# A cap of three on the loads in flight, in a decode kernel of two attention and two feed-forward layers

## The chip, the core and the metric

One core of a Trainium2 chip. The metric is the device time of one execution in microseconds (us). Compared are fast runs with fast runs; a run is called slow when it is more than 1.5% above the fastest of the same kernel. Runs that were made once only are of unknown state, and are used only for differences far above that.

## The reference, cut to what matters

```python
B, Sq, D = 4, 1, 512;  Hq, Hkv, Sk, Dh = 32, 8, 4096, 128;  F = 1792
x = x + A(layernorm(x))   # attention over k_cache, v_cache (B, Hkv, Sk, Dh), bf16
x = x + Bf(layernorm(x))  # (gelu(x @ w_gate) * (x @ w_up)) @ w_down
x = x + A(layernorm(x))   # the same caches and weights again
x = x + Bf(layernorm(x))
```

One token for each of four sequences. Each (sequence, kv head) has 1 MB of K and 1 MB of V, 64 MiB in all. There is little arithmetic on each byte, so the kernel is a stream of loads with matmuls behind it.

## The kernel before

The kernel loads K once per sequence and keeps it, turned (transposed), on the chip for both layers; V is loaded twice. That makes 64 K loads and 128 V loads of 512 KB, and 13.9 MB of weights: 114.6 MB, or 218 times 512 KB. All loads are issued in program order on one queue, that of the sync engine (SP). K and V share one pool of seven buffers, and that pool is all that limits how many K and V loads are in flight (the weights have room of their own).

```python
KV_BUFS = 7
kvin = ctx.enter_context(tc.tile_pool(name="kvin", bufs=KV_BUFS))
dq = nc.sync

def load_kv(cache, b, kvh, t, name):
    tl = kvin.tile([P, CH, Dh], BF16, name=name, tag="kv")        # 128 x 2048 bf16, 512 KB
    src = cache[b, kvh].rearrange("(p c) d -> p c d", p=P)
    dq.dma_start(out=tl[:], in_=src[:, t * CH:(t + 1) * CH])
    return tl
# ... (cut)
v = load_kv(A_v_cache, self.b, kvh, t, "v_t")
for i in range(CH):                                               # 16 matmuls per V load
    c = t * CH + i
    nc.tensor.matmul(o, lhsT=v[:, i, :], rhs=pe[:, s, c, :],
                     start=(c == 0), stop=(c == C - 1))
```

Of the kernel before, what the change touches and what calls it, by code (L numbers as in the profile page):

```python
# [15 lines left out]
P = 128  # L16
# [3 lines left out]
CH = 16  # L20
# [3 lines left out]
NB = 2  # L24
BE = 2 * NB
KV_BUFS = 7


@with_exitstack
def kernel(  # L30
# [14 lines left out]
    B, Sq, D = A_x.shape  # L45
    _, Hkv, Sk, Dh = A_k_cache.shape
    HqDh = A_wq.shape[1]
    Hq = HqDh // Dh
# [9 lines left out]
    HG = GH * rep  # L58
# [6 lines left out]
    ktp = ctx.enter_context(tc.tile_pool(name="ktp", bufs=Hkv))  # L65
    kvin = ctx.enter_context(tc.tile_pool(name="kvin", bufs=KV_BUFS))
    qbp = ctx.enter_context(tc.tile_pool(name="qbp", bufs=2))
# [20 lines left out]
    for a in range(QD):  # L88
        nc.vector.tensor_copy(
            out=sel[:, :, :, a, :],  # L90
            in_=ident_bf[:].rearrange("p (b i e) -> p b e i", b=NB, e=2))
# [4 lines left out]
    wq_sb = wts.tile([P, KD, HqDh], BF16, name="wq_sb")  # L96
    wo_sb = wts.tile([P, Hq, D], BF16, name="wo_sb")
    wg_sb = wts.tile([P, KD, F], BF16, name="wg_sb")
    wu_sb = wts.tile([P, KD, F], BF16, name="wu_sb")
    wd_sb = wts.tile([P, KF, D], BF16, name="wd_sb")  # L100
    wq_dram = A_wq.rearrange("(k p) n -> p k n", p=P)
    wo_dram = A_wo.rearrange("(i p) n -> p i n", p=P)
# [6 lines left out]
    xn_bf = state.tile([P, KD, B], BF16, name="xn_bf")  # L109

    dq = nc.sync


    def load_kv(cache, b, kvh, t, name):
        tl = kvin.tile([P, CH, Dh], BF16, name=name, tag="kv")
        src = cache[b, kvh].rearrange("(p c) d -> p c d", p=P)
        dq.dma_start(out=tl[:], in_=src[:, t * CH:(t + 1) * CH])
        return tl


# [118 lines left out]
    class Turner:  # L239
# [3 lines left out]
        def step(self):  # L243
            kvh, t = divmod(self.n, NT)
            self.n += 1
            if t == 0:
                self.kt = ktp.tile([P, G8, NB, QD, QS], FP32, name="kt", tag="kt")
                KT[kvh] = self.kt
            gt = CH // QD
            kn = load_kv(A_k_cache, self.b, kvh, t, "k_t")  # L250
            kf = kn.rearrange("p c d -> p (c d)").bitcast(FP32).rearrange(
                "p (c b i) -> p c b i", b=NB, i=QS)
            for bb in range(NB):
                nc.vector.transpose(  # L254
                    out=self.kt[:, t * gt:(t + 1) * gt, bb].rearrange("p g c j -> p g (c j)"),
                    in_=kf[:, :, bb])
# [54 lines left out]
    class Values:  # L311
# [3 lines left out]
        def step(self, count=1):  # L315
            for _ in range(count):
                if self.n == Hkv * NT:
                    return
                kvh, t = divmod(self.n, NT)
                self.n += 1  # L320
                s = kvh % GH
                if self.whole:
                    if kvh == 0 and t == 0:
                        self.ot = ps_acc.tile([P, Hkv, rep], FP32, name="ot2", tag="acc")
                    o = self.ot[:, kvh]
                else:
                    if s == 0 and t == 0:
                        self.ot = ps_ot.tile([P, GH, rep], FP32, name="ot", tag="ot")
                    o = self.ot[:, s]
                pe = self.prob[kvh // GH]  # L330
                v = load_kv(A_v_cache, self.b, kvh, t, "v_t")
                for i in range(CH):
# [3 lines that stand above are left out]
# [5 lines left out]

    def rest_weights(i):
        if i == 0:
            dq.dma_start(out=wq_sb[:, :, HG * Dh:2 * HG * Dh], in_=wq_dram[:, :, HG * Dh:2 * HG * Dh])
        elif i == 1:
            dq.dma_start(out=wq_sb[:, :, 2 * HG * Dh:], in_=wq_dram[:, :, 2 * HG * Dh:])
        elif i == 2:
            dq.dma_start(out=wo_sb[:, :Hq // 2], in_=wo_dram[:, :Hq // 2])
        elif i == 3:
            dq.dma_start(out=wo_sb[:, Hq // 2:], in_=wo_dram[:, Hq // 2:])  # L350
            dq.dma_start(out=wg_sb[:], in_=B_w_gate.rearrange("(k p) n -> p k n", p=P))
        elif i == 4:
            dq.dma_start(out=wu_sb[:], in_=B_w_up.rearrange("(k p) n -> p k n", p=P))
            dq.dma_start(out=wd_sb[:], in_=B_w_down.rearrange("(k p) n -> p k n", p=P))


    def attend(b2, qb2, b1, qb1, rstd1):
# [13 lines left out]
        for g in range(NG + 1):  # L371
# [14 lines left out]
            if b1 == 0:  # L386
                rest_weights(g)
                if more:
                    q_norm(q_proj(0, B, g * HG, HG), q1_bf[:, g * HG:(g + 1) * HG], rstd1, HG, B)
# [60 lines left out]


    x_bf = kvin.tile([P, D], BF16, name="x_bf", tag="kv")
    dq.dma_start(out=x_bf[:B, :], in_=A_x.flatten_outer_dims())
    hq0 = HG * Dh
    dq.dma_start(out=wq_sb[:, :, :hq0], in_=wq_dram[:, :, :hq0])

    xT_ps = ps_misc.tile([P, KD, B], BF16, name="xT_ps", tag="misc")
    for k in range(KD):
# [98 lines left out]
```

## Time and profile before

| | before |
|---|---|
| time, median of 3 runs (lowest to highest) | 367.79 us (366.8 to 371.84) |
| the profiled run, slow | 375.1 us, span 373.3 us |
| bytes read | 114.56 MB, 307 GB/s over the span |
| idle TensorE time before value matmuls that waited for V | 60.1 us |
| idle TensorE time called "issue" | 43.4 us |

The page of the kernel before follows. In its lines PE is TensorE, DVE is VectorE, ACT is ScalarE, POOL is GpSimd and SPq is the queue of SP; L334 is line 334 of the kernel. The trace holds 3210 landing marks, 16 for each of the 200 loads of K, V and weights; a load is counted as landed at its last mark. The parts of the page are: the busy share of the 16 DMA engines in 40 slices and the rate of each slice; the DMA queues with packets, MB and their share of the engines' time; the chain of waits by engine and by line; groups of instructions (count, busy us, mean ns, then the engine's idle time before them and what ended it); and the loads with KB and the median us from issue to landing.

```profile
span 373.3 us, 14915 instructions
...
DMA  7999999995078799999879899998888799984730
GB/s 237 421 417 383 416 375 417 395 407 228 11 253 302 234 376 363 382 313 359 288 244 386 347 329 377 358 341 275 271 332 308 265 382 413 345 311 147 248 119 2
...
q1 hardware_dynamic: 36240, 114.58, 83.7%
q8 instruction: 53, 0.87, 0.9%
...
PE 38%; DMA 29%; issue 16%; DVE 15%; POOL 1%; ACT 1%; SPq 0%; ACTq 0%; POOLq 0%; DVEq 0%
DMA v_t<-in_A_v_cache_dram 29%; PE sc L266 11%; PE ot L334 10%; DVE kt L254 7%; PE qps L166 3%; PE y L190 3%; DVE colmax L273 2%; PE y L232 2%; PE hg L204 2%; PE hu L204 2%; PE x L293 1%; PE st L128 1%; DVE sc L281 1%; POOL gmax L275 1%; PE yf L190 1%
...
L334 PE MATMUL ot<-pe,v_t 128*128 128x4 bf16 x2048 | 68.7, 167 | 77.2 <-DMA v_t<-in_A_v_cache_dram 60.1
L254 DVE STREAM_TRANSPOSE kt<-k_t 128x512 f32<-128x512 f32 x128 | 82.8, 686 | 26.9 <-DMA k_t<-in_A_k_cache_dram 16.8
L266 PE MATMUL sc<-qb,kt 128*128 128x16 bf16 x2048 | 63.0, 175 | 17.5 <-issue 13.6
...
v_t<-in_A_v_cache_dram SPq DMA_DIRECT2D x128, 512.0 KB, 7.4
k_t<-in_A_k_cache_dram SPq DMA_DIRECT2D x64, 512.0 KB, 8.8
```

The engines are near full in slices 2 to 9 and again in stretches later. The chain is a mixture: TensorE 38%, loads 29%, "issue" 16%. A V load takes 7.4 us from issue to landing, about six times what 512 KB need at 420 GB/s (the rate of the page's best slices; an estimate), and up to seven K and V loads can be in flight. The windows view of the kernel before, for the first long stretch of loads (per engine: busy us and instructions; at the end clock, DMA share, GB/s):

```profile
20.00:80.00 60.00, 17.81 (x588) 16.65 (x587) 21.89 (x49) 4.30 (x9) 3.09 (x8) 1.00 1.04 400
```

The DMA engines are full there (share 1.04) at 400 GB/s. Next, the waits view of TensorE before: who waited, for what, us in total, times, longest.

```profile
PE ot L334 <- DMA v_t<-in_A_v_cache_dram: 60.1, 35, 8.9
...
PE sc L266 <- issue: 13.6, 6, 3.2
PE ot L334 <- issue: 12.9, 7, 3.5
PE qps L166 <- issue: 10.1, 3, 3.8
```

"Issue" is idle time for which the profile shows no wait. The timeline of TensorE before shows where it lies (start us, busy us, instruction and count, and in brackets the idle time before):

```profile
119.71 0.35 PE L266 MATMUL sc<-qb,kt 128*128 128x16 bf16 x7
123.07 0.82 PE L266 MATMUL sc<-qb,kt 128*128 128x16 bf16 x25 [3.00 <-issue]
123.74 0.99 PE L334 MATMUL ot<-pe,v_t 128*128 128x4 bf16 x32
...
133.06 0.35 PE L266 MATMUL sc<-qb,kt 128*128 128x16 bf16 x7
135.94 0.82 PE L266 MATMUL sc<-qb,kt 128*128 128x16 bf16 x25 [2.53 <-issue]
```

The two stalls cut a block of 32 matmuls after its seventh, and 256 matmuls lie between them. With a weight load each, that is 512 instructions. The queue "instruction" in the page carries 53 packets and 0.87 MB, which is 16 KiB each (called a page of instructions below); TensorE's 6848 matmuls and 6848 weight loads over 53 packets are 258 instructions per packet (an estimate from the page). In the packet records each of the 22 stalls ends 1.2 to 1.6 us after the end of such a packet. I read this as TensorE having run out of instructions and waiting for a fetch. The page counts these packets on the same 16 DMA engines as the loads (0.9% of their time, against 83.7% for the loads). Last, the SP queue's own waits before:

```profile
SPq L117 <- PE ot L334: 102.1, 54, 9.5
SPq L117 <- DMA v_t<-in_A_v_cache_dram: 24.6, 17, 4.4
```

SP mostly waits until TensorE frees a V buffer; now and then it also waits for an earlier load.

### The profile page before, as it was taken

The page shows a single profiled execution, that of the slowest core. Times are in us where ns is not written, and L with a number is a line of the kernel's source. Part 1 is how long each engine was busy: PE and PEld are TensorE (multiplying, and loading weights), DVE is VectorE, ACT ScalarE, POOL GpSimd, SP SyncE. Part 2 cuts the span into 40 slices and gives each one's busy share as a digit, 9 for nine tenths or more (in the row PEclk, how much of TensorE's full clock was granted, in tenths as well). Part 3 has the DMA queues.
Part 4 walks back from the last instruction along what each step waited for, and adds up shares of the span by engine and source line. Part 5 has one row for each costly group of instructions (what it writes and reads, how often), then busy time and mean ns, then how long its engine had stood idle before and what let it go on. Part 6 is the DMA issues. An engine that isn't in the chain of part 4 may idle for free.

```text
span 373.3 us, 14915 instructions
## 1 busy us (share of the span) xinstructions
PE 204.4 (55%) x6848; PEld 193.2 (52%) x6848; DVE 160.4 (43%) x502; ACT 26.5 (7%) x70; POOL 25.1 (7%) x70
## 2 busy tenths in 40 slices
PE   0435141337765545865555657656465557678645
PEld 0334141337665445764555647655465456677635
DVE  0854423303686553321777453127745523224104
ACT  0020000000011011000011010000101000001100
POOL 0000000000010111000111110000110100002000
DMA  7999999995078799999879899998888799984730
GB/s 237 421 417 383 416 375 417 395 407 228 11 253 302 234 376 363 382 313 359 288 244 386 347 329 377 358 341 275 271 332 308 265 382 413 345 311 147 248 119 2
DMA packets 36302, 115.52 MB, mean 309 GB/s; under 512 B 3208, under 2 KB 9104, under 8 KB 36240
## 3 DMA queue, kind: packets, MB, share of 16 engines
q1 hardware_dynamic: 36240, 114.58, 83.7%
q8 instruction: 53, 0.87, 0.9%
q14 instruction: 9, 0.07, 0.0%
HBM read 114.56 MB, written 0.00 MB: 307 GB/s over the span
## 4 chain that ended last, share of the span: by engine, by line
PE 38%; DMA 29%; issue 16%; DVE 15%; POOL 1%; ACT 1%; SPq 0%; ACTq 0%; POOLq 0%; DVEq 0%
DMA v_t<-in_A_v_cache_dram 29%; PE sc L266 11%; PE ot L334 10%; DVE kt L254 7%; PE qps L166 3%; PE y L190 3%; DVE colmax L273 2%; PE y L232 2%; PE hg L204 2%; PE hu L204 2%; PE x L293 1%; PE st L128 1%; DVE sc L281 1%; POOL gmax L275 1%; PE yf L190 1%
## 5 line engine op out<-in xcount | busy, mean ns | idle before, releaser
L334 PE MATMUL ot<-pe,v_t 128*128 128x4 bf16 x2048 | 68.7, 167 | 77.2 <-DMA v_t<-in_A_v_cache_dram 60.1
L334 PEld LDWEIGHTS <-v_t 128*128 128x128 bf16 x2048 | 63.7, 105 | 82.4 <-DMA v_t<-in_A_v_cache_dram 63.8
L254 DVE STREAM_TRANSPOSE kt<-k_t 128x512 f32<-128x512 f32 x128 | 82.8, 686 | 26.9 <-DMA k_t<-in_A_k_cache_dram 16.8
L266 PE MATMUL sc<-qb,kt 128*128 128x16 bf16 x2048 | 63.0, 175 | 17.5 <-issue 13.6
L266 PEld LDWEIGHTS <-kt 128*128 128x128 bf16 x2048 | 58.9, 104 | 20.0 <-issue 15.2
L273 DVE TENSOR_REDUCE colmax<-sc 128x8 f32<-128x256 f32 x32 | 13.4, 420 | 45.0 <-PE sc L266 45.0
L293 PE MATMUL x<-raw,ident_bf 128*32 128x64 bf16 x512 | 13.4, 238 | 31.1 <-ACT raw L285 28.6
L285 ACT ACTIVATE raw<-sc 128x256 bf16<-128x256 f32 x32 | 12.3, 383 | 222.6 <-DVE sc L281 222.6
L275 POOL PARTITION_ALL_REDUCE gmax<-colmax x32 | 11.9, 371 | 229.9 <-DVE colmax L273 149.7
L166 PE MATMUL qps<-xn_bf,wq_sb 128*128 128x1 bf16 (+1 forms) x640 | 20.2, 166 | 11.3 <-issue 10.1
L293 PEld LDWEIGHTS <-ident_bf 128*32 128x32 bf16 x512 | 9.8, 118 | 31.6 <-issue 30.9
L190 PEld LDWEIGHTS <-wo_sb 128*128 128x128 bf16 x640 | 19.8, 104 | 12.2 <-issue 12.2
L166 PEld LDWEIGHTS <-wq_sb 128*128 128x128 bf16 x640 | 18.9, 104 | 11.8 <-issue 11.2
L190 PE MATMUL y<-OT_bf,wo_sb 128*128 128x1 bf16 x512 | 15.8, 165 | 9.9 <-DVE OT_bf L338 6.7
L307 POOL PARTITION_ALL_REDUCE den<-cs x32 | 12.7, 398 | 85.7 <-DVE cs L304 85.7
L338 DVE TENSOR_TENSOR OT_bf<-ot,rden 128x8 bf16<-128x8 f32 (+1 forms) x23 | 3.5, 153 | 33.7 <-PE ot L334 33.7
L281 DVE TENSOR_TENSOR sc<-sc,gmax 128x256 f32<-128x256 f32 x32 | 13.5, 422 | 8.9 <-POOL gmax L275 8.7
L298 ACT CAST pe<-x 128x256 bf16<-128x256 f32 x32 | 11.9, 372 | 33.0 <-PE x L293 33.0
L304 DVE TENSOR_REDUCE cs<-raw 128x8 f32<-128x256 bf16 x32 | 12.4, 389 | 3.8 <-ACT raw L285 3.8
L171 DVE TENSOR_TENSOR q_bf<-qps,rstd 128x8 bf16<-128x8 f32 (+1 forms) x20 | 3.3, 170 | 24.0 <-PE qps L166 23.6
L197 DVE TENSOR_TENSOR XX<-XX,y 128x4 f32<-128x4 f32 (+1 forms) x9 | 1.4, 160 | 22.5 <-PE y L232 16.0
L179 DVE TENSOR_TENSOR qb<-qe,amask 128x128 bf16<-128x128 f32 (+1 forms) x23 | 7.8, 338 | 5.6 <-PE qe L177 5.5
(50 smaller groups left out, 113.2 us busy)
## 6 DMA issues: line engine op xcount, KB each, us to landing
v_t<-in_A_v_cache_dram SPq DMA_DIRECT2D x128, 512.0 KB, 7.4
k_t<-in_A_k_cache_dram SPq DMA_DIRECT2D x64, 512.0 KB, 8.8
wo_sb<-in_A_wo_dram SPq DMA_DIRECT2D x2, 2048.0 KB, 12.5
wq_sb<-in_A_wq_dram SPq DMA_DIRECT2D x2, 1024.0 KB, 9.2
wq_sb<-in_A_wq_dram SPq DMA_DIRECT2D x1, 2048.0 KB
wg_sb<-in_B_w_gate_dram SPq DMA_DIRECT2D x1, 1792.0 KB, 17.1
wu_sb<-in_B_w_up_dram SPq DMA_DIRECT2D x1, 1792.0 KB, 13.1
wd_sb<-in_B_w_down_dram SPq DMA_DIRECT2D x1, 1792.0 KB, 17.1
```

The source lines that it names most:

```text
L166: nc.tensor.matmul(qps[:, i, :], lhsT=wq_sb[:, k, m * Dh:(m + 1) * Dh], rhs=xn_bf[:, k, bs], start=(k == 0), stop=(k == KD - 1))
L190: nc.tensor.matmul(y[:, :, dk], lhsT=wo_sb[:, i, dk * P:(dk + 1) * P], rhs=rhs, start=(first and i == h0 and dk == 0), stop=(last and i == ...
L204: nc.tensor.matmul(h[:, m, :], lhsT=w_sb[:, k, m * P:(m + 1) * P], rhs=xn_bf[:, k, bs], start=(k == 0), stop=(k == KD - 1))
L254: nc.vector.transpose(out=self.kt[:, t * gt:(t + 1) * gt, bb].rearrange("p g c j -> p g (c j)"), in_=kf[:, :, bb])
L266: nc.tensor.matmul(sc[:, s, g, :], lhsT=kt[:, g, be // 2, :, be % 2], rhs=qb[:, kvh, be].rearrange("p a h -> p (a h)"), start=(be == 0), s ...
L273: nc.vector.tensor_reduce(out=colmax[:], in_=v, axis=AX.X, op=ALU.max)
L275: nc.gpsimd.partition_all_reduce(gmax.rearrange("p s h -> p (s h)"), colmax.rearrange("p s h -> p (s h)"), P, RED.max)
L281: nc.vector.tensor_tensor(out=w, in0=w, in1=gmax[:].unsqueeze(2).broadcast_to([P, GH, G8 * QD, rep]), op=ALU.subtract)
L293: nc.tensor.matmul(x[a * QS:(a + 1) * QS, :, :, cc, :], lhsT=ident_bf[:, cc * QS:(cc + 1) * QS], rhs=raw[:, :, :, a, :], start=True, stop= ...
L304: nc.vector.tensor_reduce(out=cs[:], in_=raw.rearrange("p s g a h -> p s h (g a)"), axis=AX.X, op=ALU.add)
L307: nc.gpsimd.partition_all_reduce(den.rearrange("p s h -> p (s h)"), cs.rearrange("p s h -> p (s h)"), P, RED.add)
L334: nc.tensor.matmul(o, lhsT=v[:, i, :], rhs=pe[:, s, c, :], start=(c == 0), stop=(c == C - 1))
```

## The change

The intent was to have fewer loads in flight, so that an instruction fetch, and any load that is needed soon, does not stand behind up to seven queued loads: in the packet records of the profile, the fetch that ended each of the 22 stalls began 1.8 us or more after the previous page boundary, and up to 5.2 us after it, against 0.9 to 1.1 us with few loads in flight. Each load gets one more wait: the third last load must have landed. The other loads go through the same function; nothing else changes, and the order of the instructions on each engine is the same.

```diff
+AHEAD = 3
     dq = nc.sync
+    landed = []
+
+    def load(out, in_):
+        inst = dq.dma_start(out=out, in_=in_)
+        inst = getattr(inst, "ins", inst)
+        if len(landed) >= AHEAD:
+            tc.add_manual_dep(inst, landed[-AHEAD].name,
+                              mybir.DependencyInfo(mybir.DependencyClass.Sync, mybir.DependencyReason.DATA),
+                              reason="at most AHEAD loads in flight")
+        landed.append(inst)
 ...
-        dq.dma_start(out=tl[:], in_=src[:, t * CH:(t + 1) * CH])
+        load(out=tl[:], in_=src[:, t * CH:(t + 1) * CH])
 ... (the eight loads of weights and the one of x in the same way)
```

More of the change, by code (lines that the diff above doesn't have):

```diff
@@ L343, in rest_weights @@
         if i == 0:
-            dq.dma_start(out=wq_sb[:, :, HG * Dh:2 * HG * Dh], in_=wq_dram[:, :, HG * Dh:2 * HG * Dh])
+            load(out=wq_sb[:, :, HG * Dh:2 * HG * Dh], in_=wq_dram[:, :, HG * Dh:2 * HG * Dh])
         elif i == 1:
-            dq.dma_start(out=wq_sb[:, :, 2 * HG * Dh:], in_=wq_dram[:, :, 2 * HG * Dh:])
+            load(out=wq_sb[:, :, 2 * HG * Dh:], in_=wq_dram[:, :, 2 * HG * Dh:])
         elif i == 2:
-            dq.dma_start(out=wo_sb[:, :Hq // 2], in_=wo_dram[:, :Hq // 2])
+            load(out=wo_sb[:, :Hq // 2], in_=wo_dram[:, :Hq // 2])
         elif i == 3:
-            dq.dma_start(out=wo_sb[:, Hq // 2:], in_=wo_dram[:, Hq // 2:])
-            dq.dma_start(out=wg_sb[:], in_=B_w_gate.rearrange("(k p) n -> p k n", p=P))
+            load(out=wo_sb[:, Hq // 2:], in_=wo_dram[:, Hq // 2:])
+            load(out=wg_sb[:], in_=B_w_gate.rearrange("(k p) n -> p k n", p=P))
         elif i == 4:
-            dq.dma_start(out=wu_sb[:], in_=B_w_up.rearrange("(k p) n -> p k n", p=P))
-            dq.dma_start(out=wd_sb[:], in_=B_w_down.rearrange("(k p) n -> p k n", p=P))
+            load(out=wu_sb[:], in_=B_w_up.rearrange("(k p) n -> p k n", p=P))
+            load(out=wd_sb[:], in_=B_w_down.rearrange("(k p) n -> p k n", p=P))
     def attend(b2, qb2, b1, qb1, rstd1):
@@ L452 @@
     x_bf = kvin.tile([P, D], BF16, name="x_bf", tag="kv")
-    dq.dma_start(out=x_bf[:B, :], in_=A_x.flatten_outer_dims())
+    load(out=x_bf[:B, :], in_=A_x.flatten_outer_dims())
     hq0 = HG * Dh
-    dq.dma_start(out=wq_sb[:, :, :hq0], in_=wq_dram[:, :, :hq0])
+    load(out=wq_sb[:, :, :hq0], in_=wq_dram[:, :, :hq0])
     xT_ps = ps_misc.tile([P, KD, B], BF16, name="xT_ps", tag="misc")
```

## The prediction

> **What bounds it now.** Two things alternate. (a) The load stream: 114.6 MB on one queue. In 20–80 us the windows view shows DMA full at about 400 GB/s; landings of 512 KB loads come 1.22–1.24 us apart: 218 loads' worth x 1.24 = 271 us. The chain of waits is 29% V loads. (b) Tensor stalls called "issue": 16% of that chain; in the waits view 43 us in 22 stalls, 0.4 to 3.9 us each. In the timeline they lie 128 or 256 matmuls apart, so 256 or 512 instructions. The DMA table has a second queue, "instruction": 53 packets, 0.87 MB, so 16 KiB each. These are instruction fetches. [...]
>
> In the packet records a page's fetch starts 0.9–1.1 us after the previous page boundary when the rings are nearly empty, but up to 5.2 us after it behind several queued loads; it takes 0.95 us, and PE resumes 1.2–1.5 us after its end. Idle rings: about 3.1 us, hidden behind a page of 3.4 us; full rings: about 7 us, a stall of 3–4 us. [...]
>
> **What the change does.** Same loads, same order, same arithmetic. Each load gets one more wait: at most three in flight instead of up to seven. Most loads now go before the third last has landed, by up to 6.4 us later on.
> Gain: a lone load takes 3.2 us from issue to landing [...]. With three in flight a fetch meets an estimated 0.3–1.5 us of data instead of up to 4.3. The 43 us of stalls shrink to 5–12.
> Cost: 3 x 1.24 = 3.7 us is just above a lone load's 3.2 + 0.35 us (SP's issue): no slack. A fetch puts 0.95 us on one DMA engine; [...] now the slowest engine's landing holds up the next issue. I estimate 0.3–0.7 us per fetch where DMA bounds: cadence 1.24 -> 1.4–1.45 us.
>
> **How much is on the critical path.** First stage (to 83 us): DMA-bound; loses 2–4 us. Score/attend stages: about 13 us of stalls, 8 recovered. Stages with V loads alone between small matmuls: about 26 us of stalls, but loads there already come at 1.5 us, so about 9 recovered. Last stage 1–2. Net -15 us. Check: 218 x 1.45 us + about 31 us without loads (start, 90–101 us, tail) = 347 us as a floor; overlap is imperfect.
>
> **Predicted 353 us**, 8 in 10 within 334–371. Faster by over 2%: 0.62; within 2%: 0.26; slower by over 2%: 0.12.
>
> **What would show it.** Tensor "issue" idle falls from 43 to under 15 us; fetches start within about 2.5 us of the previous boundary. V loads' median time to landing falls from 7.4 to about 4 us. SP mostly waits for landed loads. 20–80 us drops from 400 to about 370 GB/s. Idle of values matmuls behind V loads stays near 60 us or grows.
>
> **What would make it wrong.** If shallow rings cost more bandwidth (cadence over 1.55 us), no gain. If a fetch's delay does not follow ring depth, stalls stay. If fetches cost little bandwidth and stages contract fully, below 335 us.

The 3.2 us of a lone load is the measured time. The check came to 218 x 1.45 + 31 = 347 us. "Rings" is the word of the forecast, and of the expectations below, for the loads that were issued and have not landed (full: up to seven; shallow: about three; idle or dry: few or none); the traces show packets and landings, not rings. The page of 3.4 us is 128 matmuls at 0.43 us per 16 (an estimate from the chain of the first profile). The 0.3–1.5 us of data that a fetch meets and the 0.3–0.7 us per fetch are estimates of what the change would do, not measurements. The trace before shows delays of up to 4.3 us (5.2 less 0.9) and the 0.95 us of a fetch's packet.

## The result

| | before | after |
|---|---|---|
| median (lowest to highest), 4 runs each | 369.81 us (366.8 to 372.06) | 429.43 us (427.39 to 430.47) |
| ratio of fast runs, 95% interval | | 1.161 (1.150 to 1.173) |
| read over the span of the profiled run | 307 GB/s | 269 GB/s |
| TensorE idle, value matmuls behind V loads | 60.1 us | 141.0 us |
| VectorE idle, transposes behind K loads | 16.8 us | 57.2 us |
| TensorE idle, "issue" | 43.4 us | 12.4 us |

A ratio is the mean time of one kernel's fast runs over that of the other's from the same rounds, so not quite the ratio of the medians. The profile after is fast, the one before slow; in the second profile of the kernel before (run base below) the three idle times are 58.7, 16.2 and 40.4 us. The issue time is the sum of that view's lines.

The page after, the same parts:

```profile
span 425.5 us, 14917 instructions
...
DMA  8989989897448778888888888888888988878750
GB/s 268 337 316 300 295 304 368 271 373 259 152 126 257 252 271 275 290 278 288 286 293 277 268 285 303 273 285 283 281 292 292 288 292 279 278 271 281 276 194 2
...
q1 hardware_dynamic: 36240, 114.58, 80.4%
q8 instruction: 53, 0.87, 0.8%
...
DMA 82%; PE 8%; DVE 6%; issue 2%; POOL 0%; ACT 0%; SPq 0%; DVEq 0%; ACTq 0%; POOLq 0%
DMA v_t<-in_A_v_cache_dram 49%; DMA k_t<-in_A_k_cache_dram 23%; DMA wq_sb<-in_A_wq_dram 4%; DMA wg_sb<-in_B_w_gate_dram 3%; PE sc L277 3%; DMA wd_sb<-in_B_w_down_dram 3%; DVE kt L265 3%; PE y L201 1%; PE ot L345 1%; PE y L243 1%; DVE colmax L284 1%; PE qps L177 0%; DVE sc L292 0%; PE hg L215 0%; PE x L304 0%
...
L345 PE MATMUL ot<-pe,v_t 128*128 128x4 bf16 x2048 | 72.5, 167 | 151.1 <-DMA v_t<-in_A_v_cache_dram 141.0
L265 DVE STREAM_TRANSPOSE kt<-k_t 128x512 f32<-128x512 f32 x128 | 83.0, 687 | 64.9 <-DMA k_t<-in_A_k_cache_dram 57.2
L277 PE MATMUL sc<-qb,kt 128*128 128x16 bf16 x2048 | 62.6, 174 | 7.4 <-issue 3.4
...
v_t<-in_A_v_cache_dram SPq DMA_DIRECT2D x128, 512.0 KB, 5.4
k_t<-in_A_k_cache_dram SPq DMA_DIRECT2D x64, 512.0 KB, 5.7
```

From the 13th slice to the 38th the rate is now flat at 250 to 305 GB/s, while before it swung, with 350 to 420 in the better slices. The chain is 82% loads. The median from issue to landing went down to 5.4 us, but three loads per 5.4 us is one in 1.8 us: with at most three in flight, the stream cannot be faster than three over that time. The windows, TensorE's waits and SP's waits after:

```profile
20.00:80.00 60.00, 14.17 (x470) 13.25 (x466) 19.49 (x42) 3.55 (x7) 2.34 (x6) 1.00 0.92 314
```

```profile
PE ot L345 <- DMA v_t<-in_A_v_cache_dram: 141.0, 71, 11.5
...
PE ot L345 <- issue: 5.7, 4, 2.3
PE sc L277 <- issue: 3.4, 4, 1.2
...
PE y L243 <- issue: 2.6, 2, 1.4
```

```profile
SPq L116 <- DMA v_t<-in_A_v_cache_dram: 170.1, 121, 3.9
SPq L116 <- DMA k_t<-in_A_k_cache_dram: 94.2, 62, 3.7
```

In 20 to 80 us the rate fell from 400 to 314 GB/s. The instruction stalls fell from 43.4 to 12.4 us, as intended, but the waits for V more than took their place. SP now waits 264 us for landed K and V loads.

The landings in the packet records of the two traces give the stages. "Before" is here the second profile of the unchanged kernel (run base, span 369.0 us; a single run, so of unknown state, 1.1% above the fastest).

| from the landing of load ... to ... | before | after |
|---|---|---|
| 0 to 47, first sequence and all weights | 88.3 us | 110.5 us |
| 47 to 94 | 87.7 us | 102.6 us |
| 94 to 142 | 78.6 us | 89.5 us |
| 142 to 192 | 85.8 us | 93.0 us |
| 192 to 200, the last V loads | 14.1 us | 15.3 us |

Every stage is longer, the first by most: it was bound by the load stream (in the first profile 400 GB/s from 20 to 80 us, DMA share 1.04) and had no stall to win back (TensorE has no "issue" wait in the first 108 us of that profile).

### The profile page after: what moved, and what is told of

It reads as the page before. It is cut to its first block, busy times and chain, and to the rows that moved or that the text cites. A ratio compares the mean times of both kernels' runs of the same rounds, so it can differ in the third digit from the quotient of the medians.

```text
span 425.5 us, 14917 instructions
## 1 busy us (share of the span) xinstructions
PE 208.9 (49%) x6848; PEld 195.2 (46%) x6848; DVE 162.1 (38%) x502; ACT 26.6 (6%) x70; POOL 25.2 (6%) x70
## 4 chain that ended last, share of the span: by engine, by line
DMA 82%; PE 8%; DVE 6%; issue 2%; POOL 0%; ACT 0%; SPq 0%; DVEq 0%; ACTq 0%; POOLq 0%
DMA v_t<-in_A_v_cache_dram 49%; DMA k_t<-in_A_k_cache_dram 23%; DMA wq_sb<-in_A_wq_dram 4%; DMA wg_sb<-in_B_w_gate_dram 3%; PE sc L277 3%; DMA wd_sb<-in_B_w_down_dram 3%; DVE kt L265 3%; PE y L201 1%; PE ot L345 1%; PE y L243 1%; DVE colmax L284 1%; PE qps L177 0%; DVE sc L292 0%; PE hg L215 0%; PE x L304 0%
## 5 line engine op out<-in xcount | busy, mean ns | idle before, releaser
L345 PE MATMUL ot<-pe,v_t 128*128 128x4 bf16 x2048 | 72.5, 167 | 151.1 <-DMA v_t<-in_A_v_cache_dram 141.0
L265 DVE STREAM_TRANSPOSE kt<-k_t 128x512 f32<-128x512 f32 x128 | 83.0, 687 | 64.9 <-DMA k_t<-in_A_k_cache_dram 57.2
L277 PEld LDWEIGHTS <-kt 128*128 128x128 bf16 x2048 | 58.7, 104 | 9.7 <-issue 4.9
L296 ACT ACTIVATE raw<-sc 128x256 bf16<-128x256 f32 x32 | 12.3, 384 | 247.1 <-DVE sc L292 247.0
L315 DVE TENSOR_REDUCE cs<-raw 128x8 f32<-128x256 bf16 x32 | 12.4, 388 | 3.8 <-ACT raw L296 3.8
```

The lines of the kernel that those rows point to most:

```text
L265: nc.vector.transpose(out=self.kt[:, t * gt:(t + 1) * gt, bb].rearrange("p g c j -> p g (c j)"), in_=kf[:, :, bb])
L277: nc.tensor.matmul(sc[:, s, g, :], lhsT=kt[:, g, be // 2, :, be % 2], rhs=qb[:, kvh, be].rearrange("p a h -> p (a h)"), start=(be == 0), s ...
L296: nc.scalar.activation(out=raw.rearrange("p s g a h -> p (s g a h)"), in_=sc.rearrange("p s g n -> p (s g n)"), func=ACT.Exp, scale=scale)
L315: nc.vector.tensor_reduce(out=cs[:], in_=raw.rearrange("p s g a h -> p s h (g a)"), axis=AX.X, op=ALU.add)
L345: nc.tensor.matmul(o, lhsT=v[:, i, :], rhs=pe[:, s, c, :], start=(c == 0), stop=(c == C - 1))
```

## The experiments

Theories. A: three loads of 512 KB are too few for the round trip of a load; the DMA engines fall idle between a landing and the next issue. B: three would do, were it not for the 0.95 us that an instruction fetch puts on one DMA engine each time. C: traffic of the compute engines slows the packets. Runs of the loads-only kernels are single, of unknown state, and give a wrong result on purpose; they are compared by span. lo3, lo3pe, lo3dve and lo7pe shared one chip, lo7, lo5pe, lo3big and lo6half another; the kernel before took 370.6 and 370.8 us there.

### Other depths in the real kernel

```diff
-AHEAD = 3
+AHEAD = 4      # and 5, 6, 8
```

> Four in flight instead of three. Theory A (a load's round trip, from landing of its predecessor's predecessor to its own landing, is about 5.5 us whatever the depth[...]): cadence 5.5/4 = 1.4 us where the cap binds, tensor issue stalls of 15 to 25 us, total 375 to 395 us. Theory B (only the 0.95 us that an instruction fetch puts on one DMA engine breaks the lock-step, and one more load of 1.24 us in flight covers it): cadence back at 1.25 to 1.3 us, total 345 to 362 us, below before.

> Five in flight. Theory A: 5.5/5 = 1.1 us is under the 1.24 us of full rings, so the cap hardly binds: 358 to 370 us, issue stalls 25 to 35 us. Theory B: as with four, 345 to 362 us. If the stalls of the instruction fetch matter to the time at all, one of four to six is faster than before by 1 to 4 per cent.

> Six in flight. Theory A and B: within 2 per cent of before (362 to 371 us), issue stalls 33 to 43 us, few waits of the queue for landed loads.

> Control: the added wait is there, but eight loads in flight hardly ever occur (the pool has seven buffers), so only the cost of the wait itself on the queue is left. Both theories: same as before within 1 per cent, 366 to 373 us, issue stalls about 43 us. If it is slower by several per cent, the added waits themselves cost time and neither theory is needed.

| in flight | median us | ratio to before (95%) | issue stalls, us | V load, issue to landing, us |
|---|---|---|---|---|
| 3 | 429.43 | 1.161 (1.150 to 1.173) | 12.4 | 5.4 |
| 4 | 380.85 | 1.033 (1.023 to 1.042) | 33.2 | 6.2 |
| 5 | 368.28 | 0.999 (0.991 to 1.008) | 35.5 | 6.4 |
| 6 | 369.01 | 1.001 (0.992 to 1.010) | 37.4 | 7.3 |
| 8 | 367.85 | 0.998 (0.983 to 1.013) | 33.0 | 7.5 |

The times are those of theory A; B's 345 to 362 us did not come at any depth. With eight, the added waits cost nothing that these runs resolve (0.983 to 1.013). My stalls were wrong: I expected 15 to 25 us at four and about 43 at eight. At four they are as long as at eight. They fell clearly only at three, where the stream is starved, so no depth tried has the gain without the loss, and none is faster than before. My test at five ("if the stalls matter to the time at all") thus decides nothing: with the stalls hardly changed from four to eight, these runs do not show what they cost the real kernel.

### The unchanged kernel again

> The kernel before, unchanged, for a second profile of it: the first was taken in a run above the fastest by more than 1.5 per cent. If this one is fast, its tensor issue stalls should lie at 33 to 43 us and its landings in the full stages at 1.24 us; then the drop of the stalls to 13 us in the changed kernel stands between runs of the same state. If the stalls here are under 20 us, the drop was none.

370.82 us, span 369.0 us. 25 issue stalls add up to 40.4 us (22 and 43.4 us in the slow profile), and 20 to 80 us runs at 400 GB/s. So the fall to 12.4 us does not come from the slow state. The packet records of this trace also hold what the prediction missed. From load 48 on, 26 K and V loads were issued with exactly two others in flight. Their median from issue to landing is 5.4 us (6.3 us for 25 such loads in the slow profile), not the 3.2 us plus 0.33 us of issue that I took from a load that was alone. That lone load, issued at 101.36 us in the first profile, was no clean measure either. I had split its 3.2 us into a fixed part and a full-speed transfer; the trace does not show it: the first 128 packets after its issue, nearly all its own, took 222 ns on average, while packets between 20 and 80 us took 160.

### The load stream alone

```diff
+    for b in range(B):  for kvh in range(Hkv):  for t in range(NT):     # one line here
+        for cache in (A_k_cache, A_v_cache):
+            tl = kvin.tile([P, CH, Dh], BF16, name="kv_t", tag="kv")    # seven buffers
+            load(out=tl[:], in_=src[:, t * CH:(t + 1) * CH])            # the capped load
+            for i in range(M_PER_LOAD):                                 # 1 or 34
+                nc.tensor.matmul(o[:], lhsT=tl[:, i % CH, :], rhs=ones[:], ...)
-    (all else of the kernel but the load of x and the store of the output)
```

128 loads of 512 KB. lo3: AHEAD 3, one matmul. lo3pe: AHEAD 3, 34 matmuls. lo3dve: lo3 and two transposes of each tile. lo7 and lo7pe: AHEAD 8, so that only the seven buffers limit, with 1 and 34 matmuls. lo5pe: AHEAD 5, 34 matmuls.

> Wrong result on purpose: only the stream of 128 K and V loads of 512 KB, seven buffers, at most three in flight; one matmul per load frees the buffer; no vector or scalar work and next to no instruction fetches. Theory A (closed loop of a round trip [...]): cadence 1.6 to 1.9 us, about 205 to 245 us plus start. Theory B (instruction fetches break the lock-step): without fetches cadence 1.24 to 1.3 us, 160 to 170 us plus start. Theory C (traffic of the compute engines in the on-chip memory slows the packets): as B.

> Wrong result on purpose: as the loads-only kernel with three in flight, but 34 matmuls per load instead of one, so that an instruction page is fetched every 3.8 loads, as densely as in the changed kernel. A: same cadence as with one matmul, within 0.1 us (1.6 to 1.9). B: slower than with one matmul by 0.2 to 0.5 us per load. C: little difference, since each load is read by the tensor engine only a little more.

> Wrong result on purpose: three in flight, one matmul per load, and two 128x512 vector transposes of 0.69 us each per load, as densely as the vector engine ever works in the real kernel. C: slower than without them by 0.2 us per load or more. A and B: no difference over 0.1 us per load, unless two transposes of 0.69 us are the limit themselves at 1.4 us.

> Wrong result on purpose: the loads-only kernel with one matmul per load and no cap but the seven buffers. Theory A (rings that run dry cost idle time and slow first packets): full rings, 1.24 to 1.3 us per load, 160 to 170 us in all, under one engine in ten dry between two loads. If it stays near the 1.5 us per load of the uncapped kernel with 34 matmuls, something other than the instruction fetches held that one up. If A is right, the difference of the two is what fetch stalls cost a stream in which the tensor engine is also needed.

> Wrong result on purpose: 34 matmuls per load, and no cap but the seven buffers. A and B and C: 1.22 to 1.26 us per load, 158 to 163 us plus start. Tensor issue stalls show what a full ring does to a fetch when nothing else waits: some of 3 us or more if the depth of the rings sets the delay.

> Wrong result on purpose: loads with 34 matmuls each and five in flight, between the 240.5 us of three and the 198 us of the seven buffers. If shorter rings shorten the tensor stalls without loss of bandwidth at five: stalls fall from 62 us to 40 to 50 us and the span to 180 to 192 us. If five loads already run the rings dry or leave the fetch's delay as it is: 195 to 205 us and stalls of 55 to 62 us.

| run | in flight | matmuls per load | span us | us per load (span/128) |
|---|---|---|---|---|
| lo3 | 3 | 1 | 238.5 | 1.86 |
| lo3pe | 3 | 34 | 240.5 | 1.88 |
| lo3dve | 3 | 1, and transposes | 243.8 | 1.90 |
| lo7 | 7 | 1 | 172.1 | 1.34 |
| lo7pe | 7 | 34 | 198.2 | 1.55 |
| lo5pe | 5 | 34 | 199.3 | 1.56 |

Three in flight cost 1.86 us per load with no compute and hardly any instruction fetch, the same as in the real kernel. B and C fall, since both gave lo3 at most 170 us plus start. The fetches of lo3pe add 0.02 us per load, the transposes 0.04, no more than single runs can scatter (the kernel before took 366 to 376 us). lo7 came out slightly over my 1.24 to 1.3 us; its span includes the start, and in its steady part the landings are 1.30 us apart. The pages of lo3 and then lo7 (DMA busy tenths, rate, the load queue's share of the engines' time, and the time to landing of the V loads):

```profile
span 238.5 us, 555 instructions
...
DMA  5998988988899898899898898889889898888995
GB/s 155 335 300 276 275 273 256 330 261 282 300 294 305 285 286 267 284 278 308 293 284 260 283 304 283 268 226 320 280 259 311 303 282 259 313 295 266 304 322 199
...
q1 hardware_dynamic: 18448, 67.13, 87.7%
...
kv_t<-in_A_v_cache_dram SPq DMA_DIRECT2D x64, 512.0 KB, 5.5
```

```profile
span 172.1 us, 555 instructions
...
DMA  4999999999999999999999999999999999999991
GB/s 127 313 413 413 409 408 406 410 403 411 403 411 409 408 408 410 410 370 412 410 410 411 410 409 409 408 408 408 408 408 410 410 407 410 410 409 411 409 396 77
...
q1 hardware_dynamic: 18448, 67.13, 98.9%
...
kv_t<-in_A_v_cache_dram SPq DMA_DIRECT2D x64, 512.0 KB, 8.7
```

Without the cap a load takes 8.7 us to land, longer than with it, and the stream reads 390 instead of 281 GB/s. The time to landing is not a measure of the stream; the bytes in flight over that time are: 3 x 512 KB in 5.5 us is 286 GB/s, where the page shows 281.

The packet records say more about the loss. In the steady part of lo3 a 4096-byte packet takes 203 ns on average and 8.0% take over 300 ns; in lo7 it is 164 ns and 0.1%. The records do not name the engine; with the packets assigned to engines by their times, those that start after a gap in lo3 take 500 to 700 ns on average (depending on how they are assigned), while the second to eighth packets of a load take 170 to 190 ns. A load's first and last engine report 1.9 us apart. They are 3.0 us apart in lo7, but there up to seven loads are in flight and the engines are idle for only 1.1% of the span. So with three in flight engines fall idle (12.3% of the span, see below), start again slowly (the 500 to 700 ns), and the next load is issued only when the last engine has reported (SP waited 181 us for landings in lo3). The q1 lines give both shares: 87.7% of 238.5 us is 23% more packet time than 98.9% of 172.1 us, and idle time grew from 1.1% to 12.3%; together they make the 1.39 between the spans. The real kernel has the same mark: from 20 to 80 us a packet took 160 ns before (0.1% over 300 ns) and 187 ns after (6.1%).

lo7pe is the one case in which the price of the fetch stalls can be estimated. I had expected 158 to 163 us plus start, and it took 198.2. TensorE's issue waits in lo7pe, then in lo5pe:

```profile
PE o L111 <- issue: 61.7, 31, 3.5
```

```profile
PE o L111 <- issue: 63.2, 32, 3.7
```

Without the cap, 34 matmuls per load instead of one made the stream 26 us longer (198.2 against 172.1). TensorE was busy for 123.5 us and stalled for 61.7 us, together 185.2 of the 198.2 us, so TensorE and no longer the queue set the pace. Its busy time alone would fit into the 172.1 us of the loads; so the stalls probably cost most of the 26 us, but no run had 34 matmuls without fetches, and this is argued and not shown. A cap of five leaves the stalls as they are (I had given that the second place). By the landings, lo7pe without a cap had only 4.5 loads in flight on average, since SP waited 129.4 us for TensorE to free buffers; with the cap it was 4.2. With three in flight (lo3pe) the waits view has no "issue" at all, but TensorE waits 102.9 us for loads.

### Bytes or loads in flight

```diff
-CH = 16            # lo3big: 1 MB per load, AHEAD 3, 64 loads
+CH = 32
-load(out=tl[:], in_=src[:, t * CH:(t + 1) * CH])       # lo6half: two of 256 KB, AHEAD 6
+for lo in (0, CH // 2):
+    load(out=tl[:, lo:lo + CH // 2], in_=src[:, t * CH + lo:t * CH + lo + CH // 2])
```

> Wrong result on purpose: loads only, three in flight, but loads of 1 MB (64 of them), so 3 MB in flight instead of 1.5. If the bytes in flight decide (round trip about 5.4 us against 7.4 us of queued data): 2.5 to 2.75 us per MB, 165 to 182 us in all. If each load costs a fixed extra of about 0.6 us (what three loads of 512 KB show over 1.24 us): 3.1 us per MB, about 200 us. If the number of loads in flight alone sets the rate: 3.66 us per MB, about 240 us.

> Wrong result on purpose: loads only, six in flight, each half as large (256 KB), so the same 1.5 MB in flight as with three of 512 KB. If the bytes in flight decide: 225 to 245 us, as with three of 512 KB. If the number of loads in flight decides: 165 to 180 us, as without a cap.

lo3big took 164.3 us, 2.57 us per MB, just below what I gave; lo6half 220.0 us. The page of lo3big:

```profile
span 164.3 us, 299 instructions
...
DMA  5999999999999999999999999999999999999993
GB/s 141 417 429 429 419 417 427 427 421 417 421 427 423 419 417 427 427 419 419 423 427 421 419 417 425 425 419 421 423 427 417 419 423 427 423 419 419 425 425 163
...
kv_t<-in_A_v_cache_dram SPq DMA_DIRECT2D x32, 1024.0 KB, 7.4
```

Three loads in flight are enough when they are 1 MB each (409 GB/s over the span), and six are too few when they are 256 KB each (305 GB/s; three of 512 KB read at 281, seven at 390). In these runs the bytes in flight decide to first order. The packets changed size too, but a packet of 8192 bytes took 314 ns in lo3big, against 164 ns for 4096 bytes in lo7, only 4% less per byte. lo6half is 8% better than lo3, a little outside what I gave for bytes alone, so finer pieces helped somewhat (220.0 us against 238.5).

### One engine, and seven

```diff
-load(out=tl[:], in_=src[:, t * CH:(t + 1) * CH])
+load(out=tl[:17, :8], in_=src[:17, t * CH:t * CH + 8])     # lo3one, lo7one: 17 rows of 2 KB
+load(out=tl_flat[:17, :960], in_=flat[:17, ...])           # lo3e1: 17 rows of 1920 B
+load(out=tl_flat[:119, :960], in_=flat[:119, ...])         # lo3e7: 119 rows, seven engines
```

One landing mark per load in the packet records of the first three, and seven in lo3e7, confirm the number of engines.

> Wrong result on purpose: loads only, three in flight, each of 17 rows of 2 KB, which go through one DMA engine (about 1.3 to 1.4 us of transfer there), so a landing waits for one engine and not for the last of sixteen. If the loss at three in flight is mostly that a landing waits for the last of sixteen engines, each of which runs dry at other times: at most 0.15 us over the same loads uncapped. If one engine alone already runs dry because the round trip is longer than three transfers: 1.7 us per load or more, some 0.3 us or more over uncapped. The memory is also less loaded here, so a small loss does not by itself tell skew from load.

> Wrong result on purpose: the same one-engine loads with no cap but seven buffers, as the yardstick: one engine always full, about 1.3 to 1.4 us per load, and under one load in ten that finds the engine dry.

> Wrong result on purpose: three one-engine loads in flight as before, but rows of 1920 bytes, so that one load is about 1.3 us of transfer on its engine, close to the 1.24 us of the real loads. If one engine's round trip fits into three transfers of that length: still no idle time, no packet over twice the usual, about 1.3 us per load. If the 1.40 us of the earlier one-engine loads was just long enough: 1.4 us per load or more with gaps on the engine.

> Wrong result on purpose: the same on seven engines (119 rows of 1920 bytes), three in flight, about 170 GB/s asked for. If the loss comes with the number of engines that a landing waits for, or with the load on the memory, it shows here in part: 1.4 to 1.7 us per load, first packets after a dry ring over 300 ns. If it is there only when all sixteen engines ask: 1.3 us, as with one engine. If packets stay at their usual length and time is still lost, it is the wait for the last engine alone.

lo3one took 182.0 us and lo7one 181.8, both 1.42 us per load: on one engine, three in flight lose nothing. At 34.8 KB per load that is only about 25 GB/s (an estimate). lo3e1, with shorter transfers of 1.37 us per load, took 175.3 us; after the first 8 us no packet was longer than 92 ns in any of the three (the usual is 82 to 85). lo3e7 took 224.1 us, 1.75 us per load, a little over the worst I had given, at only 131 GB/s: 4.0% of its packets took over twice the median, the longest 2.3 us. So the prediction's sum, three transfers against one round trip, fits a load on one engine. It fails for loads on sixteen (1.86 us in lo3 against 1.34 in lo7), and the seven engines lost time as well, at a third of lo7's rate: seventeen packets of the usual 79 ns need 1.34 us (an estimate), and a load took 1.75. Two things stay open. A seven-engine run without a cap was not made, and it is not known why the first packets are slow. The runs cannot part the wait for the last engine from the slow packets either, as both came together.

## Why the prediction was wrong

The prediction was 353 us, with 12% for slower by over 2%; the changed kernel took 429.43 us.

- **Right: what the stalls are, and that they shrink at three in flight.** Issue idle fell from 43.4 us (40.4 in the second profile) to 12.4 us (forecast: 5 to 12, "under 15"). SP did mostly wait for landed loads (264 us). The median start of a fetch after the previous page boundary fell from about 2.8 to about 2.0 us (boundaries 6 to 52), and in the loads-only kernels it was 1.7 us in lo3pe and 3.2 us in lo7pe. "Within about 2.5 us" did not hold for all: a tenth came over 3.2 us later. How much of the fall comes from fewer loads in flight is not shown: TensorE also waited 81 us more for V loads, and such waits may hide fetches (lo3pe, which is lo7pe with the cap, has no "issue" wait beside its 102.9 us of waits for loads, while lo7pe has 61.7 us beside 12.2).
- **Wrong: the cost term.** The step that failed reads "3 x 1.24 = 3.7 us is just above a lone load's 3.2 + 0.35 us" and its result "cadence 1.24 -> 1.4–1.45 us". Measured was 1.87 us per load (between the 61st and the 187th K or V load of the changed kernel). The size of the loop, not the fetches, was the error: with two others in flight a load takes 5.4 us to land. The same sum with the measured cadence, 218 x 1.87 + 31, is 439 us, above the measured 429, so it was not quite the floor that it was called. Nor was 1.24 us the cadence of the whole kernel: between the same loads the kernel before took 1.62 us, and 218 x 0.25 = 54 us (an estimate) is near the 60 us that were lost.
- **Wrong for the same reason:** "V loads' median time to landing falls ... to about 4 us" (5.4), "20–80 us drops ... to about 370 GB/s" (314), first stage "loses 2–4 us" (22 us). "Idle of values matmuls behind V loads stays near 60 us or grows" left room for the growth, but not for its size (141.0 us).
- **Wrong cause of the loss:** I charged it to instruction fetches, 0.3 to 0.7 us each. The run with loads alone (lo3) has one fetch and takes 1.86 us per load, as much as the changed kernel (1.87).
- **Where the gain went.** About 30 us of stalls did vanish, but every stage became longer, with loads as 82% of the chain, so none of it shortened the time; waits for V (81 us more, TensorE) and K (40 us more, VectorE) took its place.
- **The text's own warning** was the right one: "If shallow rings cost more bandwidth (cadence over 1.55 us), no gain." The cadence was 1.87 us.

## What to carry to other kernels

Before capping the loads in flight, take the time to landing from loads that already had that many others in flight, not from a lone one, and divide the capped bytes by it: in these runs that was about the rate left. Here three loads are 1.57 MB, and over 5.4 us that is 291 GB/s, where the page after shows 250 to 305 in its flat part; five loads, 2.6 MB, were enough for the whole kernel. The old trace had the number (6.3 us in the slow profile). Here a wait of some 30 us that the cap removed elsewhere was worth nothing, because the stream itself had become the limit.
